# Four interleaved attention layers on one core: a new table of orders, engines and PSUM banks

## The chip, the cores and the metric

The kernel runs on one core of a Trainium2 chip. The core has five engines that run side by side, each through its own list of instructions in order: TensorE (PE in the profile; its weight loads are PEld), VectorE (DVE), ScalarE (ACT), GpSimd (POOL) and SyncE (SP, which here only issues DMAs). They wait for one another through semaphores. PE writes to PSUM, which has eight banks; DVE and ACT read PSUM and write SBUF; POOL works in SBUF alone. The metric is the device time of one execution in microseconds, as the median of several runs.

## What is computed

The input x has 2048 tokens of 512 features. Four residual layers follow one another, A, B, A, B, each on a layernorm of x. All have 32 heads of 16 features.

```python
def _A_ref(x, wqkv, wo):                      # linear attention
    q, k, v = ...                             # x @ wqkv, split into heads
    phi = lambda t: jnp.where(t > 0, t + 1, jnp.exp(t)) + 1e-6
    pq, pk = phi(q), phi(k)
    kv = jnp.einsum("bhsd,bhse->bhde", pk, v)
    z = jnp.einsum("bhsd->bhd", pk)
    num = jnp.einsum("bhqd,bhde->bhqe", pq, kv)
    den = jnp.einsum("bhqd,bhd->bhq", pq, z)[..., None] + 1e-6
    return (num / den) @ wo

def _B_ref(x, wqkv, wo):                      # sliding window, W = 256
    q, k, v = ...
    scores = jnp.einsum("bhqd,bhkd->bhqk", q, k) * (Dh ** -0.5)
    mask = (i - j >= 0) & (i - j < W)
    p = _softmax(jnp.where(mask, scores, -1e9))
    return jnp.einsum("bhqk,bhkd->bhqd", p, v) @ wo

x = A_x
x = x + _A_ref(_layernorm(x), A_wqkv, A_wo)
x = x + _B_ref(_layernorm(x), B_wqkv, B_wo)
x = x + _A_ref(_layernorm(x), A_wqkv, A_wo)
x = x + _B_ref(_layernorm(x), B_wqkv, B_wo)
```

## The kernel before

The tokens are cut into 16 tiles of 128. The residual stream stays in SBUF (`xres`) from the first load to the last store. `Plan.build` (L236) writes the whole program down as a graph of 2532 operations (`Graph.add`); an operation is one instruction, or a group of matmuls that goes by one name. Each names the engine or engines that may run it, what it reads and writes, and the PSUM tiles that it uses. A tile of PSUM is one bank.

The program has these parts, and work of one part is mixed with that of its neighbours:

- *First layer A, keys* (`layer_a_keys`): for each tile the layernorm (`norm`, L330 to L334: statistics on DVE, the inverse root in two POOL instructions, the scaling `xn` on DVE), a transposition, the key matmuls (`k`, L369) and phi: exponential on ACT (L392), two DVE instructions (L393, L394). Gram matrices of keys and inputs are summed over all 16 tiles (L444). Queries (`q`, L383) go through phi as well.
- *Barrier* (`barrier`): the sums over all tiles are complete (`kvm`, L486), the matrix M that joins them with the output weights is formed, and the denominators (`den`, L506; `rec`, L510; `recb`, L511; `spread`, L519; `pqd`, L526) are divided out.
- *First pass* (`middle(2)`): for each tile the output of layer A (`aout`, L369) is added to the residual (`res`, L537), normalised, transposed, and the layer-B queries, keys and values are made (`bq` and `bk`, L383; `bv`, L369; their copies `bqe`, L358, `bke`, L554 on ACT and L555 on DVE, `bve`, L358). Keys and values are laid out anew by two DMAs each (`kd`, L563; `vd`, L582). Then attention: scores of near blocks (`b_scores`, L599, 256 queries wide, two head groups at once), exponentials on ACT (`ex`, L609, 128 x 1024) and the diagonal mask on DVE (`mk`, L615); scores of the far edge (`b_far`, L632), exponentials (L641) and the edge mask (`mf`), either on POOL (L649) or on DVE (L650); values (`b_values`, L674), division (`rcp`, L685; `div`, L686), transposition of the output (`oT`), output matmul (`bout`) and residual. Keys and values (`a_k`, `a_v`, with the copy `ve`, L358) of the second layer A are made as its input appears.
- *Second barrier* and *second pass* (`middle(3)`): the same for layers three and four. Finished tiles leave by DMAs on POOL's queue (L783), the last by SP's.

The table's layernorm and output transposes are DMAs on SP's queue (L340) but for the first tiles of a part and the last one, which PE transposes through PSUM (L346) and ACT or DVE copies (`Te`, `oTe`, L353).

A score group uses four PSUM tiles at once, two for each of its two exponentials; an exponential reads two banks in one instruction.

What sets the order is a table. `place` (L88) decodes `TABLE` (L795): two bytes for each of the 2532 places give the operation that stands there in one global order, then one byte for each operation its engine, then one byte for each PSUM tile its bank. Each engine runs its operations in the global order; `synchronise` (L123) adds the semaphore waits that the dependencies need, among them that a tile that takes a bank comes after all uses of the tile that held it. So the table fixes every queue, SP's and POOL's too. The lines that pick an operation's place, engine and bank are these:

```python
order = [ops[raw[2 * k] + 256 * raw[2 * k + 1]] for k in range(n)]
o.eng = ("PE", "ACT", "DVE", "POOL", "SP")[raw[2 * n + o.i]]
x.banks = [raw[3 * n + k]]
```

Of the kernel before, what the change touches and what calls it, by code (L numbers as in the profile page):

```python
# [11 lines left out]
P = 128  # L12
D = 512
DH = 16
S = 2048
T = 16
# [196 lines left out]
class Plan:  # L213
# [372 lines left out]
    def b_scores(self, j, b, fs, key):  # L586

        K = self
# [4 lines left out]

        def put(e):
            m = None
            for i, f in enumerate(fs):
                for gq in range(4):
                    rows = slice(32 * gq, 32 * gq + 32)
                    m = e.matmul(K.ps(ps[gq])[:, ns * i:ns * i + ns], K.kB[rows, j % 4, 2 * f + b, :, :], K.XQ[rows, f, q:q + ns], start=True, stop=True, tile_position=(32 * gq, 0))  # L599
            return m  # L600
# [5 lines left out]
        for h in range(2):  # L606
            def ex(e, h=h):
                i = bass_view(K.PS[:, ps[2 * h].banks[0], :], [[512, 2], [ns, n], [1, ns]])
                return e.activation(out(2 * h, 2, ns), i, ACT.Exp, bias=0.0, scale=0.25)  # L609

            self.on("ACT", "ex", ex, key + 0.01 * h, act(2 * ns * n), wr=[("P", sl, f, b, h) for f in fs], rd=[("P", sl, f) for f in fs], ps=[ps[2 * h], ps[2 * h + 1]])
# [7 lines left out]
    def b_far(self, j, key):  # L619
# [3 lines left out]

        def put(e):
# [171 lines left out]
    r"c-rk(1Jq?nlFo<>WR`8)wr$(CZQHhO+qP|2wQYCpd+)ER>6z)7?d|Q|b9PU~|G&KV2EL5=B3_<%jfrF;8#GZ(6a&T@Hqi{3=q9BR6T`$bsZ44U",  # L796
    r"%cL=}O&pWf#5L)Rnmi_+NpJF+_@=$dVDg##CZkDUI+#JGqse3{nyIFk>0}C+X(qENXq-uCN}435kntv|8Emqc#wMKEX_}bCX1SSenwo4TndxkX",
    r"m>Fh;X=b{ZT_(IaZL*uLCWk3yikrgbuIXlSn&zgv*=_EbnI@6xVa}LbW|qlnhMJY;7gNr(Fsn>YGt8VdtIcq8-?TKn%tvO88DYws(xxPwGb7C?",
    r"6B&w_*=CO!ZO)rH=2w&4d~7b52d0l1W9FK@rnebuJ~1!NJ~PjJYSx;EX1-ZxN|<q`j7bXX%_FnGj5h{0n9s~YlMFVRYUXou(PW29X1^(GqQGU7",
    r"!W=N0%@vaz4w_OB6|S1crZhY;Dd3O+Xbgu<4TG@BJT*tmQIis)!58M4Nd>u0eRJJBHx*13^QCEJu9+9+D^tmof#_i2YZC)<Kuz<FA!uzFaza^n",  # L800
    r"$FwoIpd1J^fp1M)lN(ZlLLHL_(m*>?*QAB-jDrZKDWrqSCOyQ2dL|b1HMLD_=x5?Ud8lRjo48N`JWPa&kQWA+d=MWhK~Xc%#Do0M$Yg{JP#Gqe",
    r"MP{)n01Zq*SYir6LsJ+gnn`A<X$F&EnW+jbpbFH5de9MS!(_9?R5w#h9jI!ynodw3wwVUd5E{XD(;1GL=FkOpn3m8Ux<M;w3+<pQw1(rR4RnAT",
    r"=7i}1lVJ*UhovwTmcdDL2ByKg<}56SZE({}hf`(-yl1w<Ot@uMz${n^=U_Ihg73|0m;*bYC%kVKz#7;IYhfWAhudZm?1Emf8&1F;SPXOFB-}Cc",
    r"Afo9FKbXBRAI?J`*attFjnEG^!8-WBEP<cQX1D--;Ua{CQ*a4BH0vQ8{%peIWe5-b;R;m12rvK+!3H=C5g`I@fk$uzDq<vf0!Lv#RKf#r8XiML",
    r"{1C3fRyYVB!$)uzjzJ`>jFIskM8Rut1*771xDTH~G`xzR!&A5cpFkD73D@v5cnDST8C1htFbN;P3#g8h@eX_e@o@@1hZL9quVX5Vj_*JXjDZO;",
    r"B__d`*bozAGQ5F}a4O!0FJT}w#-un62f@4W6*R@^7z<}$226yhF*e@BjF=p6;d_t?;$SAs4DZ8COoLy;Ec^hnKwA6;vfyAyhjlP3WX1IO6V%0Q",
    r"P!qFZW^9J_uogDK7ML9uV{Kf5&G9yN!ljr4?_g)li7oMG$c0_-7s!pRups^lv#~YK!I$t9+u&UM7M`KOt{4vizlXbs_#ETnJ^T(VcEkHP4+(qV",
    r"4=^7KVO#8udGJRljP)@eR)Zqg0INe@EQ;;0J=TB)xB_cJ0w{((u{f^64p;ygYk}ZO?1%}W1S+n<)z}O3<610<z0qMQT!#;^5B9}Gum#uSVBCO-",
    r"VJmLKB(M=ZF2jeo376w$e1t<_JC??wPzIyfvKZYChY?T?ci=E60y{B=9fIX?DDJ|dFbs>qhZxh=wjbectYc%@;TYTQ!H+SH9f8GRFV?jq@mm~)",
    r"`*4AcYrn@55YH~O`|&%hXWzx-_9%XW@8Kdl8sEo$xY$0mi*Skk0Y}18`wrH(&ujxb3I<?*Y-q<|3LD>kfXi%3`y~#<WB4^bw}bFFCa_=O2|R#}",  # L810
    r"?5B7TM?+(~+<t?fVM2QdGuY4ZG5&}zY({$+U*Jjn2{YLz_ywl1@7SMlEWT?O;xCxij>98pZF74HGu!ca8gtn9Y&zS*PQcW5BA&sVHkD0p6WRA|",
    r"V%yT@vU%)T%wm(+y!ISswfSsEo6R<{*=;AA+cvfNE!k$av+ZixcC!Vn*e<raJ&$TH;IG)jUc`bnnSF_uu#LTpZLP6|th0S>Ve4%>8_t%r8*P6J",
    r"c9ZRA2U@i4ZFt+$4zerk0K3`tvV-k5o7DEUrR;V)#73~CZ6CYCma)6+P}{+lwY%*a`++TIciOeKyxn6f*dlhF9cGK#y>_J?ZY$bi_K+Q6E7?`{",
    r"h>d7V*wr?Y9cK^QG4Q1=ZpT7o`<2~lCqOFt+HSF_X*{&D<KURBY+KtX_JmDCRcusS)sD2s?T5CSU2m(~kL(6J+NP!Pc7jbuAKRlgJ)N@??I@dp",
    r"+EWM0NEhrR`-#m&pW2i5yxnIf+p%_vooe^nj`W%R$zHNw*aP;IJ!pTno#?dv#eQec*ex{8cBb#`S-X|G(69Eg%}rzMHu}NlAxn8F8%?)NUFk=g",
    r"ox0IWOLWoZpl__wb~4nR9POaYw3C25Wg(<p^tlx(Kw0UE{ni$ut2P|Xum$OwooS2Ebvw(3r=oPj&bBvg1e#-S*<w_IBGNY$i3(Fi>P^L|58bwv",
    r"s0`h)ed${&OC{(#ia{l*GL@t6X(;ue;gpZcQ&0MVO3{y$pLSCf8b&`+Y3fB)X(UynyS6%wrV(_{)}@~*CXJ$46q)YZ*ffB0QWSb%2hu}(l=e_m",
    r"8brq^4o#)wRF4MJ7@9_LDH_G2TvVSP+4wY_hENT9Y!gsTicSe>u5Cc`Y%MxK4XHmJr1`cEO{9L*hz`+Mnnb_Q6FZI?(+rwSP3RPjr@b_RPSX@h",
    r"MEmFrC8qs!j*?JQnn`Er0yU$gG>ekadAdcj3HT(<q1%Lfkrq*H61IGYu95Nyx<Sq9E;(*N*Xa^nrj~S*!gDKHOjjr(U!^6~nj&yyUP||98Aav$",
    r"w4Czs3W~xHXeGtwhm@Zq@pFp9tLRrMz%MB-&!yF5I62Luc$|WwaU1eHpHfnMK0<9N0WYMpe3;tNIZnur=mjkx=Ew97CE{?rhTf$ow3dk9qxX3o",  # L820
    r"CFc(~I<Kdc{60OS4RoGUa18!{I&n<?kUr$%9E(5V#9We}(#M>HOK@RM%}Kc+cjjbVgwyaf?!wo(D3{{${1I)W3j8q@<4shWEAnP4!-Y5%-{8tz",
    r"mM?H6uFB>3BH!dHe2IJWE$+kB_!GL#pHg4$&T08G>c>6#bNYnS@fXyCKjrjXoj>Cm+>0~taPG?e`Ewr0HTer3z#}*#*Wye(m<MtL&dguZARfx2",
    r"_$$i7mw5<(O<8#<U*Y9k!w%zRT${V`3a)9davdJcb$JXo<gr}KHsXa`pU3fH9?xI$B5ustxE^QcCY*ztGRQ`5#$WMf&dJSr32$PQuek-U<=p%Y",
    r"uj7`yh4b)w{+1_jUf#eHITugj?|3VJ&y#r@ujC*2N1no~cq(t_X}p75@oH|*cX&Fl;TilB-{pI}ldUwD`@D-E@NVA2E#x8Z<<|U&_i-DZ$1}MD",
    r"&*#UypWE^QCOOE5cow(g!#tax@DYB>3z+37pW<UYhv)KfKF!a#BR}U8e3D=A8GeV~<@fk!ZYFspkNm>L<X0{t;ib4lkfQRE3rPtv5>Z47O96=_",
    r"`6RNGl>DMnN(zdT($Z2|Nf~J^V`ZGglr~aUdP^T^E90e|#FF;XSC&W==^*{2qb!w9;w7r|mkBaJVoNs}D9fa~Oq9+tNG3@S2`7VPvUHK2GDPA?",
    r"Ihi6|rI!qqxDri<NqLzn!)1g_laW$EmP<t$CDCQNtdJ_QQpU(CsVp;OmduvXGE*wae5oo6WR9$sW3o{0$Xq!gG32f+lC5%F?#VpaCEMh_ES5bI",
    r"MYqcuiK@Hhft-?u5=}plM{-)CYZ)!8XC#K6lusq5K9&z9mX^~e@|k=t@g%m!m-3oecF0GvRuV`Yt)Tm4uT<1^@`db|N}5nM$a>i+N#uZ>m8bHt",
    r"B$8*6R1V5Uc`lb^lN^#{a#*fNa@i~|<Q+L8Tja7Fl`rL8`9$LCR}xRJ%KLIouE}|cuV2fLazPU4Mfq7OYf`-~-$*k3NfK&uttN@|S4pYW#b_1%",
    r"R=$(8@{7Ebbn?BtCpDz5{vhcEG?k{%dYVB}Yeu;tH>JL&QPEq1npjoSs@1AW>NK6QR@3mBUTdh=>RMAXXf~~-Q#FT9(~KHUhv;<8u8nl4HqlI)",  # L830
    r"Q-^70ZLGsJmqySmnny=yR*k45b(E%%+!{$!%4jX5sU)wC(d?31a!6!NBl)z57S`IDUz=)9X{H6Vffm(F(n1?*X2~T5^|mC@+|pdzX&oJ_?X`op",
    r")Z%(pi|IH$r&*+?bky-$N6za6tt%6?mSmMqI!SBG9__5zWUqG761q=kX-VC$v-NW=rC;bA?W(=Bw0^1eq>oP416p6Y=@dPvy>*@*(yz3YF3`E!",
    r"TEEuA`i*wiBicZ|)%n^++v+m?PSdy*+Cyh(PfhC<Y7_UpF4umV&Rx=`F1@>=i?qM?)n;z7Ue*k5l`heln$aEAmAYCpxutqco4XUbMq9XRdR$w&",
    r"liJGN(5pH?*Xlq$rPp<n4$>d=jBe4J`lGgXr*)lXcAIsu{-pPGz24Vt`m=7(3;IBR(T#dhAL*|O?ul+!bhq@eS|=`xd#Jb7xu?2S^SV2#?yiP&",
    r"`CNGSO!K=o?zu*AwcHD3m({(awOvG)&3&Za?a(?dyL(r6D!KQxo{Qvmsd4XXEca5|x;U<#`%ojh_Aa*T=c2gXn!`nP{asGi)zx*m+yEENb#u|(",
    r"#~Rmtpxxak8p9=WpK1q}$0czcT}+qTeWvkTCzse2a`D|jSJ)+R1zl2C#1(S|TtZjEC3g*_s7vM=NpaU$=C~$O&dqgArMz3~=DBsQf-C8Ix%sY?",
    r">+Ke}^{%vA==!)tu97R`Qn=1;v8&=zy0UJG>+7z#RIaj{<gU7ku8T|Urno`wnj7pUyQ*%RyY8yF?QV!0>Z-dNZil<+M!BA@hP&mQuj$4(?{B-Q",
    r"ZmGND!uio|m|Nz;`w?!MTj6@R<!+@L?l!qqu87~_#=4?@wTs|Kx`_U%tM7KYNPe^1=Zg7f?tmNTwz}tTyxZ?0`*&S&AI0x-@3{%CgrDekyOREW",
    r"SISR!huj`_*X?zOU1@*M9dv7419#sYai`n{_knBZHoDU;sz2%)xoG~3`_?sf(fu*^y*uvCxd-k$cf!5nzH}$uL-)d+bzi#~?!0^CX1cH3hi;aO",
    r";XiVZ-48CN|Hj4jv)#uomjBho^Do^e?nhU~$M-)u<J0+{T^#?Z`^9DO=s$DmeIgG&f&bi9^<TKeKB2$hF1n2ViA&;>`Ag3FYCeT8>#O^6KDJNp",  # L840
    r"lln})yszLh`-(oL@8c`^EWVcS>udW|KCAEN>-b!rd}W{8v#;x`_|#r}9^cHT@#?erw7!MU?(_QQzMik?bNHOTfv@3P`O7Z9Z|xWRmVSxP=iB)D",
    r"exPsb+xbDhp>OY(`oVsz@8BExj((hP?8p0|zKI{;hxh`1xG(4@_@=&)ALhIJiGGqF;n(>7zOY~GNBYTrlwaqk_)dPbpXxjNF@C+D=DYY6e!5@g",
    r"d-xfCrSIx{`gy*WU*%`|ZhpC+<#+hizPI1tcln)uqo3`!_)UJZ-|FZ1qkgyF=I8slet|#kxBFv$p+D*O_|yJ`Kjkm_Gk&kX<QMtN{;J>S&-(rT",
    r"n!oO^_yhi&zu|BC^ZtUr<?s62{+_?%ANc$Jp?~Bb`-A?8KjfeJr~a^i?vHr-JFx-5z}s5jrP>(4z!JKIso-~1_CJw7hVoA;`oFFLfY5DFFj!&m",
    r"FTiSG3CKTR(S)G{z29&W_$PX;q2E#9E5$##VMq~Jf@y?OLHx&i{JR*$zsLO}2=;#%0seCYi~n7OKf(k2`yBqc3ivNm@jHe536S66^LOS4{>y~?",
# [168 lines left out]
```

## Time and profile before

| | |
|---|---|
| median of three runs | 431.54 us (431.0 to 432.18) |
| span of the profiled execution | 428.2 us |
| mean granted TensorE clock in it | 0.986 |
| PE busy | 392.7 us (92%), 7471 matmuls recorded |
| DVE busy | 356.2 us (83%), 796 instructions |
| ACT busy | 347.4 us (81%), 433 |
| POOL busy | 128.6 us (30%), 223 |
| first near exponential of the first pass | starts at 69.04 us |
| first near exponential of the second pass | starts at 269.68 us |

The span runs from the first to the last instruction of the profiled execution; the runs' times also take in what lies around it. How busy each engine is over the span, in 40 equal slices, tenths of a slice, with the granted TensorE clock below:

```profile
PE   8899999999899999999999999999889979997775
...
DVE  6998899998998799887887789998798699875564
ACT  2423547999899999999998164999999999999992
POOL 4789322101240233130503303212144324332000
PEclk9999999999999999999999999999999999999968
```

ACT's row shows the parts of the program: it fills up when the first pass begins, about slice 7, falls off at slices 22 to 24, the second barrier, and is full again until the end. [...]

Waits are read from the list of who waited for whom; the longest on the engines that compute, apart from POOL's, are these (engine, line, what ended the wait: total us, times, longest):

```profile
ACT tE L392 <- PE ps L369: 20.6, 19, 2.2
DVE rc L685 <- PE ps L674: 15.0, 29, 1.5
PEld ps L599 <- ACT pb L609: 14.9, 31, 1.3
ACT tE L392 <- PE ps L383: 14.0, 10, 3.8
DVE pb L615 <- ACT pb L609: 11.6, 21, 2.1
```

### The profile page before, as it was taken

What the parts mean: (1) busy time and instruction counts of PE and PEld (TensorE: products, weight loads), DVE (VectorE), ACT (ScalarE), POOL (GpSimd) and SP (SyncE); (2) the same over time, 40 slices, a digit from 0 to 9 for tenths busy, and PEclk for the clock granted to TensorE, in tenths of its full rate; (3) what the DMA queues carried; (4) which work ended last, traced back from release to release, by engine and by line L of the source; (5) the groups of instructions that cost most, each with busy time, mean ns of one, the idle gap of its engine ahead of it and who ended that gap; (6) DMA issues with size and microseconds to landing.
All of it is one profiled execution on the core that took longest, in us unless ns stands there. A gap on an engine that the chain in (4) does not pass through costs nothing.

```text
span 428.2 us, 17035 instructions
## 1 busy us (share of the span) xinstructions
PE 392.7 (92%) x7471; PEld 257.9 (60%) x7548; DVE 356.2 (83%) x796; ACT 347.4 (81%) x433; POOL 128.6 (30%) x223
## 2 busy tenths in 40 slices
PE   8899999999899999999999999999889979997775
PEld 3445676766465566565565768585657746765544
DVE  6998899998998799887887789998798699875564
ACT  2423547999899999999998164999999999999992
POOL 4789322101240233130503303212144324332000
PEclk9999999999999999999999999999999999999968
DMA  7933016432153533453324000452434522553222
GB/s 248 269 74 87 2 42 160 117 90 70 39 111 64 103 103 77 91 112 55 95 47 65 19 2 26 114 120 63 113 62 106 116 77 77 116 133 102 64 52 51
DMA packets 66978, 37.81 MB, mean 88 GB/s; under 512 B 48248, under 2 KB 61816, under 8 KB 66904
## 3 DMA queue, kind: packets, MB, share of 16 engines
q1 hardware_dynamic: 66176, 34.75, 34.7%
q0 software_dynamic: 720, 1.97, 1.3%
q8 instruction: 59, 0.97, 1.0%
q14 instruction: 15, 0.12, 0.1%
q10 hardware_dynamic: 8, 0.00, 0.0%
HBM read 6.29 MB, written 2.10 MB: 20 GB/s over the span
## 4 chain that ended last, share of the span: by engine, by line
PE 42%; ACT 35%; DVE 16%; issue 4%; DMA 3%; POOL 1%; POOLq 0%; ACTq 0%
ACT pb L609 23%; PE ps L369 14%; PE ps L383 11%; PE ps L674 7%; ACT pb L641 6%; PE ps L599 4%; ACT vp L609 3%; DVE stats L330 2%; DVE XQ L526 2%; DVE vp L394 2%; ACT tE L392 1%; DVE tE L393 1%; DVE vp L334 1%; DMA xT<-xn 1%; DVE xres L537 1%
## 5 line engine op out<-in xcount | busy, mean ns | idle before, releaser
L609 ACT ACTIVATE pb<-ps 128x1024 bf16<-128x1024 f32 (+2 forms) x224 | 207.0, 1039 | 7.5 <-PE ps L599 6.1
L674 PEld LDWEIGHTS ps<-vB,pb 128*128 128x128 bf16 x2560 | 78.0, 96 | 13.0 <-DVE pb L615 2.8
L674 PE MATMUL ps<-vB,pb 128*128 128x34 bf16 x2560 | 83.6, 178 | 2.0 <-DVE pb L615 1.1
L392 ACT ACTIVATE tE<-ps 128x512 bf16<-128x512 f32 x64 | 38.8, 609 | 41.0 <-PE ps L369 20.6
L383 PE MATMUL ps<-xT,wBp 128*128 128x128 bf16 x1024 | 69.5, 219 | 2.1 <-DMA xT<-xn 0.8
L332 POOL TENSOR_SCALAR ve<-mv 128x1 f32<-128x1 f32 x64 | 16.6, 260 | 174.0 <-DVE mv L331 172.4
L383 PEld LDWEIGHTS ps<-xT,wBp 128*128 128x128 bf16 x1024 | 58.9, 98 | 14.8 <-issue 3.6
L615 DVE TENSOR_TENSOR pb<-pb,tri 128x512 bf16<-128x512 bf16 x112 | 48.0, 436 | 12.3 <-ACT pb L609 11.6
L599 PE MATMUL ps<-XQ,kB 32*128 32x256 bf16 (+2 forms) x1024 | 50.1, 270 | 6.9 <-ACT pb L609 3.4
L641 ACT ACTIVATE pb<-ps 128x1024 bf16<-128x1024 f32 x50 | 49.4, 1061 | 1.1 <-PE ps L632 1.0
L369 PE MATMUL ps<-wA,XQ 128*128 128x512 bf16 x177 | 46.3, 380 | 3.6 <-DVE vp L394 0.7
L537 DVE TENSOR_TENSOR xres<-ps,xres 128x512 bf16<-128x512 f32 x63 | 43.0, 685 | 7.3 <-PE ps L369 6.4
L649 POOL TENSOR_SCALAR_AFFINE_SELECT pb<-pb 128x1024 bf16<-128x1024 bf16 x30 | 35.3, 1175 | 38.5 <-ACT pb L641 37.3
L330 DVE BATCH_NORM_STATS2 stats<-xres 128x6 f32<-128x512 bf16 x64 | 43.1, 680 | 2.6 <-DMA xres<-in_A_x_dram 2.0
L333 POOL TENSOR_TENSOR rs<-ve,negh 128x1 f32<-128x1 f32 x64 | 37.5, 586 | 5.3
L383 PE MATMUL ps<-XQ,wA 128*128 128x128 bf16 x512 | 36.1, 219 | 0.4 <-DVE vp L394 0.2
L599 PEld LDWEIGHTS ps<-XQ,kB 32*128 32x128 bf16 x1024 | 15.5, 92 | 33.8 <-ACT pb L609 14.9
L369 PE MATMUL ps<-M,XQ 128*128 128x512 bf16 x115 | 31.7, 381 | 4.0 <-DVE XQ L526 1.6
L383 PEld LDWEIGHTS ps<-XQ,wA 128*128 128x128 bf16 x512 | 30.6, 98 | 7.7 <-DVE vp L394 1.2
L369 PE MATMUL ps<-wBo,oT 128*128 128x512 bf16 x104 | 30.1, 395 | 3.4 <-ACT pb L609 0.9
L369 PE MATMUL ps<-wBv,xT 128*128 128x512 bf16 x106 | 30.7, 381 | 2.7 <-issue 0.8
L369 PEld LDWEIGHTS ps<-wA,XQ 128*128 128x128 bf16 x192 | 16.1, 98 | 21.5 <-ACT XQ L353 1.7
(109 smaller groups left out, 541.2 us busy)
## 6 DMA issues: line engine op xcount, KB each, us to landing
vB<-vS SPq DMA_DIRECT2D x64, 136.0 KB, 2.5
kB<-vp SPq DMA_DIRECT2D x64, 128.0 KB, 2.2
out_dram<-xres POOLq DMA_DIRECT2D x15, 128.0 KB, 2.3
wA<-in_A_wqkv_dram SPq DMA_DIRECT2D x3, 512.0 KB, 5.9
xres<-in_A_x_dram SPq DMA_DIRECT2D x2, 512.0 KB, 4.9
pb<-in_B_wqkv_dram SPq DMA_DIRECT2D x1, 1024.0 KB, 9.0
xres<-in_A_x_dram SPq DMA_DIRECT2D x3, 256.0 KB, 4.9
wAo<-in_A_wo_dram SPq DMA_DIRECT2D x1, 512.0 KB, 7.4
```

The lines of the kernel that those rows point to most:

```text
L330: self.on("DVE", "stats", lambda e: e.bn_stats(K.stats[:, t, :], K.xres[:, t, :]), key, dve(512), rd=[("xres", t)], wr=[("stats", t)])
L333: self.pow = self.on("POOL", "pow", lambda e: e.tensor_tensor(K.rs[:, t, :], K.ve[:, t, :], K.negh[:], ALU.pow), key + 0.03, (640, 690), r ...
L369: m = e.matmul(K.ps(ps), lhs(c), rhs(c), start=c == 0, stop=c == 3)
L383: m = e.matmul(K.ps(ps)[:, f * P:(f + 1) * P], w(c, f), xT(c), start=c == 0, stop=c == 3)
L392: self.on("ACT", "E", lambda e: e.activation(K.tE[:, s, :], K.ps(ps), ACT.Exp, bias=0.0), key, act(512), wr=[("tE", s)], ps=[ps])
L537: self.on("DVE", "res", lambda e: e.tensor_tensor(K.xres[:, t, :], K.ps(po), K.xres[:, t, :], ALU.add), key, dve(512), rd=[("xres", t)], w ...
L599: m = e.matmul(K.ps(ps[gq])[:, ns * i:ns * i + ns], K.kB[rows, j % 4, 2 * f + b, :, :], K.XQ[rows, f, q:q + ns], start=True, stop=True, ti ...
L609: return e.activation(out(2 * h, 2, ns), i, ACT.Exp, bias=0.0, scale=0.25)
L615: return e.tensor_tensor(x, x, K.tri[:, 0, :].unsqueeze(1).unsqueeze(1).to_broadcast([P, 4, n, 64]), ALU.mult)
L641: return e.activation(far(h), i, ACT.Exp, bias=0.0, scale=0.25)
L649: return e.affine_select(out=x, in_=x, compare_op=ALU.is_ge, fill=0.0, base=-2, pattern=[[0, 16], [-2, 64]], channel_multiplier=1)
L674: m = e.matmul(K.ps(ps)[:, 34 * u:34 * u + 34], K.P((b // 2) % rp)[:, gq, f, o:o + P], K.vB[:, (b // 2) % 4, b % 2, r, :], start=i == 0, s ...
```

## The change

The whole `TABLE` is replaced by another one of the same form: another global order, other engines for 41 operations that may run on more than one, and other PSUM banks. The graph of operations, their instructions and their dependencies through data stay. Engines change so: the far-edge mask from DVE to POOL 15 times and from POOL to DVE 10 times; the copies `Te` (3), `bqe` (2), `Me`, `bve` and `oTe` (1 each) from DVE to ACT; `ve` (3), `bke` (2), `ge` and `recb` (1 each) from ACT to DVE. After it ACT has 433 operations of the graph for 432, DVE 789 for 795, POOL 224 for 219; PE and SP keep theirs.

Besides, the exponentials of `b_scores` and `b_far` no longer assume that their two banks lie side by side: a small function `pair` takes the distance from the table, and the far exponential's output is written with one dimension more.

```diff
@@ b_scores
+        pair = lambda two, free: bass_view(K.PS[:, two[0].banks[0], :], [[512 * (two[1].banks[0] - two[0].banks[0]), 2]] + free)
...
             def ex(e, h=h):
-                i = bass_view(K.PS[:, ps[2 * h].banks[0], :], [[512, 2], [ns, n], [1, ns]])
+                i = pair(ps[2 * h:2 * h + 2], [[ns, n], [1, ns]])
                 return e.activation(out(2 * h, 2, ns), i, ACT.Exp, bias=0.0, scale=0.25)
@@ b_far
+        pair = lambda two, free: bass_view(K.PS[:, two[0].banks[0], :], [[512 * (two[1].banks[0] - two[0].banks[0]), 2]] + free)
...
-        far = lambda h: bass_view(K.P(sl)[:, 2 * h, 0, 256:320], [[704, 8], [384, 2], [1, 64]])
+        far = lambda h: bass_view(K.P(sl)[:, 2 * h, 0, 256:320], [[2816, 2], [704, 4], [384, 2], [1, 64]])
         for h in range(2):
             def ex(e, h=h):
-                i = bass_view(K.PS[:, ps[2 * h].banks[0], :], [[128, 8], [64, 2], [1, 64]])
+                i = pair(ps[2 * h:2 * h + 2], [[128, 4], [64, 2], [1, 64]])
                 return e.activation(far(h), i, ACT.Exp, bias=0.0, scale=0.25)
@@ module
 TABLE = (
-    r"c-rk(1Jq?nlFo<>WR`8)wr$(CZQHhO+qP|2wQYCpd+)ER>6z)7?d|Q|b9PU~|G&KV2EL5=B3_<%jfrF;8#GZ(6a&T@Hqi{3=q9BR6T`$bsZ44U",
...
+    r"c-qxi1Gp_ol8%Us$jE%QZQHhO+qP}nwr$(C{o1y>-_|*|dv|B2r*~$yzuDb7=T>D!2L3-HGEdb7hy?~>Lo^_W4rw7B!~ldi5EtS>0Z0!SAR`FGhXjxiG",
...
```

In the old order SP issues the input and weight loads as x0, x1, key weights (A), x2-3, x4-5, query weights (A), x6-7, x8-11, x12-15, value weights (A), output weights (A), layer B's query and key weights, then the first transposes; in the new one as x0, x2-3, x1, key weights, x4-5, x6-7, query weights, x8-11, the first transpose, x12-15, layer B's query and key weights, value weights, then further transposes, with the output weights of A among them.

## The prediction

> **What bounds the kernel now.** I read the page's totals first, then busy time by stretch, then the chain that ended last, then single lines. I cut the span where ACT's work changes: to the first exponential of the first attention pass (69 us), its last (235), the first of the second pass (269.5), its last (419.3).
>
> ```profile
> 69.00:235.00 166.00, 156.10 (x3159) 101.12 (x3191) 145.12 (x332) 157.79 (x190) 41.46 (x68) 1.00 0.38 84
> 235.00:269.50 34.50, 33.34 (x566) 25.61 (x569) 29.27 (x67) 15.06 (x27) 8.13 (x15) 1.00 0.09 25
> 269.50:419.30 149.80, 134.83 (x3052) 91.60 (x3072) 117.15 (x255) 145.78 (x168) 40.29 (x57) 0.97 0.39 93
> ```
>
> Columns: stretch, length, then busy us (instructions) of PE, PE's weight loads, DVE, ACT, POOL, then clock, DMA share, GB/s. ACT is busy 95% of the first attention pass and 97% of the second, and idles over half of the boundary between them, where PE is 97% busy. ACT sets the passes, PE and DVE the rest. The chain agrees, except that PE takes over in the second half of the first pass:
>
> ```profile
> PE 42%; ACT 35%; DVE 16%; issue 4%; DMA 3%; POOL 1%; POOLq 0%; ACTq 0%
> ```
>
> The main ACT work and the price of an exponential:
>
> ```profile
> L609 ACT ACTIVATE pb<-ps 128x1024 bf16<-128x1024 f32 (+2 forms) x224 | 207.0, 1039 | 7.5 <-PE ps L599 6.1
> ...
> L599 PEld LDWEIGHTS ps<-XQ,kB 32*128 32x128 bf16 x1024 | 15.5, 92 | 33.8 <-ACT pb L609 14.9
> ```
>
> Exponentials of 1024 columns take 1.06 us each but start 0.90 us apart when back to back (the chain of waits has "126.17 7.34 ACT pb L609 x8", 0.92 each); a break costs the idle time and some 0.16 us of lost overlap. Score matmuls in turn wait 14.9 us for ACT to free PSUM banks: the loop score, exponential, free bank, score is tight on both sides.
>
> **The change part by part.** Both tables were read out beside each other (two bytes an operation for the order, one for its engine, one a tile for its bank). All 2532 operations stay. Of 858 PE groups 435 keep their predecessor on the engine, of 795 on DVE 197, of 432 on ACT 131, of 219 on POOL 81, of 228 on SP 31; 816 of 997 bank numbers change. 41 operations change engine. The sum goes by what this moves into or out of the bounding stretches.
>
> *The access patterns.* In both tables every pair of score banks is adjacent (all 156 groups), so the new stride equals the old 512, and the far output [2816 x 2][704 x 4] is the same walk as [704 x 8]. Cost nil; nothing need hide it. If the extra dimension cost 10 ns in each of 312 exponentials, they being the bound, it would be 3 us.
>
> *ACT's work inside the passes.* Prices are start-to-start times of back-to-back rows: about 0.49 us for a phi exponential, 0.61 for L554's key copy, 0.48 for L358's plain copies, 0.54 for the V copies, 0.20 for L511. First pass: one phi exponential fewer (-0.49), one key copy fewer (-0.61), three layer-A value copies fewer (-1.43), two query copies (+0.96) and one V copy (+0.54) more: -1.0 us. Second pass: one key copy (-0.61) and L511 (-0.20) fewer: -0.8. The boundary gets +1.7 us of ACT work, hidden by PE (ACT is busy 15 of 34.5 us there); uncovered it would cost 1.7. **Term -1.8.**
>
> *Score groups with little cover.* For each group I counted the ACT work ordered between the exponential that frees its last bank and the one that reads it. With a whole exponential or more between, the trace shows 0.03 us of idle a group in the first pass; with half, 0.17; with none, 0.55 (second pass 0.02, 0.09, 0.40). Counts, first pass: none 4 to 6, half 20 to 10, whole 47 to 52: +1.10 - 1.69 + 0.13 = -0.46. Second pass: none 3 to 2, half 6 to 7, whole 66 to 69: -0.40 + 0.09 + 0.05 = -0.26. Eight breaks fewer at 0.16 each: -1.28. **Term -2.0**; bounds 0 (what is no longer ACT's wait becomes PE's) and -4.
>
> *DVE, and masks to POOL.* L650 masks on DVE (0.60 us start to start) become L649 on POOL 15 times and the reverse 10 times, net five, so DVE sheds 3.0 us in all, 2.9 of it in the first pass after the other swaps. DVE holds 16% of the chain: 2.9 x 0.16 = -0.5. Against it stands what POOL's mask does to DVE:
>
> ```profile
> L649 POOL TENSOR_SCALAR_AFFINE_SELECT pb<-pb x30: 1136/1147/1659, 98.7 to 381.9; 128x1024 bf16<-128x1024 bf16 x30
> ...
> L334 DVE TENSOR_SCALAR xn<-xres,mv,rs x48: 320/405/1239, 58.0 to 369.5; 128x512 bf16<-128x512 bf16 x48
> ...
> L615 DVE TENSOR_TENSOR pb<-pb,tri x112: 359/416/1376, 73.2 to 415.2; 128x512 bf16<-128x512 bf16 x112
> ```
>
> Durations are minimum, median and maximum in ns. The 1239 ns L334 and the 1376 ns L615 began beside a POOL mask: three L334 then took 1.2 us for 0.40, some L615 0.8 to 1.4 for 0.42, two L393 0.6 and 0.8 for 0.28. All such stretching, twelve cases in the timeline, sums to 6.9 us over 35 POOL masks, 0.20 each. At that rate five more masks cost 1.0 us of DVE. Laying each mask at its place in the orders, DVE operations of these kinds that begin beside one go from 19 to 45; at 6.9 / 12 = 0.57 us for each of 26 more that is 15 us of DVE. On the path at DVE's 16%: +0.2 to +2.4; uncovered at most +15. Placement in an order is rough, so I take +0.7. **Term, both: +0.2.** The Trainium skill ("SBUF — State Buffer", Who interferes with whom) says that one of them that takes the shared port pair holds it for its whole instruction and the other fully blocks, for a DVE operation with two SBUF inputs or in a two-port mode; "Perfetto Trace Analysis", Optimizing Scalar/DVE Operations, warns that offloading between the two might not help. Taken literally, moving a 0.60 us mask onto a 1.15 us one that can block DVE is a loss, and this term would be near its upper end; the trace, where most POOL masks stretch nothing, makes it small.
>
> *Transposes with less cover.* SP's transposes (L340) land at best 2.4 us after their input is ready, in the middle 3.0, in a quarter of cases over 4.0:
>
> ```profile
> L340 SPq DMA_TRANSPOSE xT<-xn x28: 1189/1256/2755, 60.1 to 379.0; - x28
> ...
> DMA to landing us min/median/max: 2.4/2.6/5.1
> ```
>
> I counted the work of the busiest engine ordered between the release of a layernorm transpose (its input and everything that SP queues ahead) and the first matmul that reads it. Before, the shortest is 3.3 us and five are under 4.0. After, four are under 3.0 (2.4, 2.4, 2.6, 2.8) and eleven under 4.0. Against a 3.0 landing the shortfall is 0.6 + 0.6 + 0.4 + 0.2 = 1.8; against 4.0 it is 8.9 where it was 2.0, 6.9 more. Three of the four lie where PE holds the chain, but the matmuls have some slack behind other work as well; I take half, **+0.9**; bounds 0 and +6.9. Queued behind a late one on PE are the next token tile's matmuls, and behind them ACT. The attention outputs' transposes get longer cover (under 4.0: 3 to none), which offsets some.
>
> *The head.* PE work ordered before the first scores goes from 54.4 to 54.0 us and DVE's from 54.0 to 53.7, so -0.3. But on SP the key weights now come behind another 256 KB of input, about 1 us at the 270 GB/s of the first 20 us, and the loads of tiles 12 to 15, of layer B's weights and of layer A's value weights stand behind the first transpose. The other input loads run ahead of it and DVE begins on them; bounds -0.3 to +1.5, **term +0.2**. In the tail PE's last 26 groups are the same but for one score group; nil.
>
> **Sum:** -1.8 - 2.0 + 0.2 + 0.9 + 0.2 = -2.5. The profiled span is 428.2 us; the runs have 431.0 to 432.2, so 3.3 lie around it at the median and are unchanged. 428.2 - 2.5 + 3.3 = **429.0 us**.
>
> **Rivals.** *Larger gain.* The passes lose 316 us of stretch less 293.5 us of ACT work at back-to-back prices (151.4 and 142.1), 22 us. The bank numbers now rotate over all eight (66% of score tiles lay in the first four, now 54%), so waits could shrink also where I count equal cover. If four tenths of the 22 went: -9, 422.5 us. For it: cover rises in the first pass. Against: in the second it doesn't. *No change:* in the second half of the first pass the chain is PE's, and PE's work there is 141.2 us in both; ACT's relief goes nowhere, -0.8 in the second pass is left, transposes give it back: 431.5. *Slower: transposes late on SP.* Short cover at 33, 129, 156, 162, 171, 227 and 240 us stalls PE's queue with DVE's xn (L334) stretched by POOL masks just before. At the 4.0 us landing, +6.9 instead of +0.9, with DVE at -0.5 + 2.4 and the score term at nil: -1.8 + 1.9 + 6.9 + 0.2 = +7.2, so 438.7; it decides against the change, other terms as forecast, once late transposes cost over 3.4 us. For it: before, no transpose had such short cover, and all PE waits on them sum to about 2 us. Against: in the passes PE has 10 to 15 us of slack behind ACT.
>
> **How the numbers follow.** Forecast 0.42, larger gain 0.17, no change 0.11, slower 0.30. A measurement can tell 0.3%, about 1.3 us, from none. Nearly all of the forecast case lies beyond that: faster 0.58, same 0.12, slower 0.30. The forecast's own range is 425 to 430; the range to reach eight in ten goes from 420.5 to 436.
>
> **What would show it.** Right: ACT idle before L609 under 6 us; ACT busy 1 to 2 us less in the passes; PE's idle before L383 and L369 for a transpose at 3 us or less. Wrong: more than 5 us of such waits; L334's mean well over its 446 ns with L649 beside it; the first exponential later than 70 us; or a chain in which ACT's share rises though its work fell.

## The result, and the profile after

| | before | after |
|---|---|---|
| median of four runs | 431.86 us (431.0 to 433.36) | 443.52 us (442.75 to 447.94) |
| ratio, 95% interval | | 1.029 (1.0234 to 1.0345) |
| span of the profiled execution | 428.2 us | 439.9 us |
| mean granted TensorE clock | 0.986 | 0.984 |

The new table is 2.9% slower. The forecast was 429.0 us with a range to 436; the time lies outside it, beyond the rival that had the transposes late (438.7). Medians here and below are of all runs; two of the kernels with loads moved had one run each in a slower state of the chip, which their ratios leave out.

Inserted lines move the numbers: the near exponential L609 is now L611, its scores L599 L601, the diagonal mask L615 L617, the far exponential L641 L645, POOL's mask L649 L653, the values L674 L678, the division L685 and L686 L689 and L690. First the busy time by stretch of the kernel after, cut at its own first and last near exponentials (columns as in the prediction):

```profile
0.00:70.39 70.39, 63.22 (x632) 37.16 (x633) 59.80 (x136) 27.81 (x49) 36.44 (x80) 1.00 0.49 123
70.39:241.21 170.82, 161.70 (x3222) 102.91 (x3221) 146.95 (x324) 156.95 (x187) 51.22 (x76) 0.99 0.36 82
241.21:276.46 35.25, 33.79 (x548) 25.04 (x544) 30.67 (x64) 17.33 (x32) 7.80 (x15) 1.00 0.08 24
276.46:430.70 154.24, 138.52 (x3068) 91.24 (x3068) 120.85 (x258) 145.71 (x166) 39.90 (x56) 0.98 0.41 91
```

Against the stretches before, the head is 1.4 us longer, the first pass 4.8, the boundary 0.8, the second pass 4.4. ACT's work in the passes fell by 0.9 us and its idle time rose: 170.8 - 157.0 = 13.9 us in the first pass (8.2 before), 154.2 - 145.7 = 8.5 in the second (4.0). DVE works 3.7 us longer in the second pass (120.85 for 117.15), in three instructions more. The chain that ended last, by engine:

```profile
PE 45%; DVE 23%; ACT 13%; DMA 9%; POOL 5%; issue 5%; SPq 0%; POOLq 0%; DVEq 0%
```

ACT held 35% of it; now 13%. DVE went from 16 to 23, DMAs from 3 to 9, POOL from 1 to 5. The exponentials still do the most work, but they are fed late. Their group, and that of the far mask on POOL (busy time, mean ns, then idle time before and what ended most of it):

```profile
L611 ACT ACTIVATE pb<-ps 128x1024 bf16<-128x1024 f32 (+2 forms) x224 | 208.3, 1023 | 15.9 <-PE ps L601 14.5
...
L653 POOL TENSOR_SCALAR_AFFINE_SELECT pb<-pb 128x1024 bf16<-128x1024 bf16 x37 | 44.7, 1209 | 30.0 <-ACT pb L645 28.3
```

ACT waits 15.9 us before L611 where it waited 7.5. In the list of waits PE's weight loads wait less for ACT's banks (12.9 us for 14.9): the loop between scores and exponentials is a little less tight from that side. The waits of interest in the kernel after (`XQ` holds the transposed inputs of layer A, `xT` those of layer B, `oT` the transposed attention outputs), and the row of the page for PE's matmuls on `XQ`:

```profile
ACT pb L611 <- PE ps L601: 14.5, 25, 1.6
PEld ps L601 <- ACT pb L611: 12.9, 23, 1.6
...
PE ps L383 <- DMA xT<-xn: 2.9, 5, 0.9
...
PE ps L369 <- DMA oT<-o: 1.6, 2, 1.3
...
L369 PE MATMUL ps<-wA,XQ 128*128 128x512 bf16 x192 | 48.5, 380 | 5.1 <-DMA XQ<-vp 2.7
```

PE's matmuls now wait 2.7 + 2.9 + 1.6 = 7.2 us for transposes (7.5 with the smaller entries), where it was 1.4; PE's weight loads wait for the same landings. Layer B's transposes land no later than before:

```profile
L340 SPq DMA_TRANSPOSE xT<-xn x28: 1190/1270/2517, 60.5 to 395.6; - x28
...
DMA to landing us min/median/max: 2.4/2.5/4.6
```

Their worst case went from 5.1 us to 4.6, so what is short for them is the cover. The attention outputs' transposes have the median that they had too (2.5 us for 2.6), but the longest takes 5.5 us for 4.1. The other view that moved is that of single DVE lines (minimum, median, maximum in ns):

```profile
L334 DVE TENSOR_SCALAR xn<-xres,mv,rs x48: 321/403/1328, 58.3 to 390.0; 128x512 bf16<-128x512 bf16 x48
...
L393 DVE TENSOR_SCALAR tE<-tE x64: 229/282/1976, 9.6 to 319.1; 128x512 bf16<-128x512 bf16 x64
...
L617 DVE TENSOR_TENSOR pb<-pb,tri x112: 360/415/1390, 74.9 to 427.0; 128x512 bf16<-128x512 bf16 x112
```

Medians are as before, maxima are not rare any more: 22 DVE instructions beside one of the 40 POOL masks are stretched, that is, they take longer than the median of their kind, by 15.4 us in all (11 of L617, 5 of L334, 4 of L393, 2 masks on DVE). Before it was 12 instructions and 6.9 us beside 35 masks. Two places of the timeline of the kernel after (start, length, engine, line, and in brackets the idle time before it with what ended it):

```profile
310.98 1.98 DVE L393 TENSOR_SCALAR tE<-tE 128x512 bf16<-128x512 bf16 x1 [0.45 <-ACT tE L392]
312.99 0.69 DVE L394 SCALAR_TENSOR_TENSOR XQ<-ps,tE 128x512 bf16<-128x512 f32 x1
313.59 0.25 DVE L689 RECIPROCAL rc<-ps 128x16 f32<-128x16 f32 x1
313.88 0.42 DVE L690 TENSOR_TENSOR o<-ps,rc 128x256 bf16<-128x256 f32 x1
...
311.63 2.38 POOL L653 TENSOR_SCALAR_AFFINE_SELECT pb<-pb 128x1024 bf16<-128x1024 bf16 x2
...
314.36 0.40 PE L601 MATMUL ps<-XQ,kB 32*128 32x256 bf16 x8 [1.58 <-DVE o L690]
...
314.81 1.94 ACT L611 ACTIVATE vp<-ps 128x1024 bf16<-128x1024 f32 x2 [1.49 <-PE ps L601]
...
383.04 1.72 DVE L617 TENSOR_TENSOR pb<-pb,tri 128x512 bf16<-128x512 bf16 x2
...
383.35 2.42 POOL L653 TENSOR_SCALAR_AFFINE_SELECT pb<-pb 128x1024 bf16<-128x1024 bf16 x2
```

The first place is the loss in small: L393 takes 1.98 us for its 0.28, so phi, reciprocal and division behind it on DVE are 1.7 us late; PE, whose next scores wait for that division, stands still for 1.58; ACT, which waits for those scores, for 1.49. (L393 begins ahead of the recorded start of the mask, beside a POOL store's issue; spans on POOL are rough.) At 383 us two diagonal masks take 1.72 us for 0.83, the second lying wholly beside POOL's mask.

### The profile page after: what moved, and what is told of

It is laid out like the page before. It is cut to its first block, busy times and chain, and to the rows that moved or that the text cites. A ratio compares the mean times of both kernels' runs of the same rounds, so it can differ in the third digit from the quotient of the medians.

```text
span 439.9 us, 17188 instructions
## 1 busy us (share of the span) xinstructions
PE 401.9 (91%) x7548; PEld 259.5 (59%) x7548; DVE 362.1 (82%) x790; ACT 348.7 (79%) x434; POOL 135.9 (31%) x228
## 4 chain that ended last, share of the span: by engine, by line
PE 45%; DVE 23%; ACT 13%; DMA 9%; POOL 5%; issue 5%; SPq 0%; POOLq 0%; DVEq 0%
PE ps L369 16%; PE ps L383 11%; PE ps L678 9%; ACT pb L611 7%; PE ps L601 5%; DVE stats L330 3%; DVE xres L537 3%; ACT vp L611 3%; DMA xT<-xn 2%; DVE pb L617 2%; DMA oT<-o 2%; DVE xn L334 2%; ACT pb L645 2%; DVE tE L393 2%; DVE XQ L526 2%
## 5 line engine op out<-in xcount | busy, mean ns | idle before, releaser
L611 ACT ACTIVATE pb<-ps 128x1024 bf16<-128x1024 f32 (+2 forms) x224 | 208.3, 1023 | 15.9 <-PE ps L601 14.5
L678 PEld LDWEIGHTS ps<-vB,pb 128*128 128x128 bf16 x2560 | 78.0, 96 | 16.6 <-issue 6.2
L678 PE MATMUL ps<-vB,pb 128*128 128x34 bf16 x2560 | 83.0, 178 | 5.2 <-DVE mv L331 1.6
L332 POOL TENSOR_SCALAR ve<-mv 128x1 f32<-128x1 f32 x64 | 15.7, 245 | 203.7 <-DVE mv L331 202.9
L392 ACT ACTIVATE tE<-ps 128x512 bf16<-128x512 f32 x64 | 37.9, 606 | 32.3 <-PE ps L369 16.5
L601 PE MATMUL ps<-XQ,kB 32*128 32x256 bf16 (+2 forms) x1024 | 50.4, 272 | 9.4 <-ACT pb L611 2.6
L617 DVE TENSOR_TENSOR pb<-pb,tri 128x512 bf16<-128x512 bf16 x112 | 51.9, 468 | 3.2 <-ACT pb L611 2.8
L653 POOL TENSOR_SCALAR_AFFINE_SELECT pb<-pb 128x1024 bf16<-128x1024 bf16 x37 | 44.7, 1209 | 30.0 <-ACT pb L645 28.3
L369 PE MATMUL ps<-wA,XQ 128*128 128x512 bf16 x192 | 48.5, 380 | 5.1 <-DMA XQ<-vp 2.7
L645 ACT ACTIVATE pb<-ps 128x1024 bf16<-128x1024 f32 x50 | 49.4, 1054 | 1.9 <-PE ps L636 1.8
L333 POOL TENSOR_TENSOR rs<-ve,negh 128x1 f32<-128x1 f32 x64 | 38.3, 598 | 5.3
L601 PEld LDWEIGHTS ps<-XQ,kB 32*128 32x128 bf16 x1024 | 15.7, 93 | 36.8 <-ACT pb L611 12.9
L369 PE MATMUL ps<-wBo,oT 128*128 128x512 bf16 x124 | 34.5, 388 | 2.7 <-DMA oT<-o 1.6
L369 PE MATMUL ps<-wBv,xT 128*128 128x512 bf16 x128 | 35.1, 381 | 0.9 <-ACT vp L611 0.5
L369 PE MATMUL ps<-M,XQ 128*128 128x512 bf16 x128 | 33.2, 381 | 1.7 <-DVE XQ L526 0.8
L383 PE MATMUL ps<-XQ,wA 128*128 128x128 bf16 x512 | 34.6, 219 | 0.1
```

The costliest lines, as they stand in the source:

```text
L333: self.pow = self.on("POOL", "pow", lambda e: e.tensor_tensor(K.rs[:, t, :], K.ve[:, t, :], K.negh[:], ALU.pow), key + 0.03, (640, 690), r ...
L369: m = e.matmul(K.ps(ps), lhs(c), rhs(c), start=c == 0, stop=c == 3)
L383: m = e.matmul(K.ps(ps)[:, f * P:(f + 1) * P], w(c, f), xT(c), start=c == 0, stop=c == 3)
L392: self.on("ACT", "E", lambda e: e.activation(K.tE[:, s, :], K.ps(ps), ACT.Exp, bias=0.0), key, act(512), wr=[("tE", s)], ps=[ps])
L617: return e.tensor_tensor(x, x, K.tri[:, 0, :].unsqueeze(1).unsqueeze(1).to_broadcast([P, 4, n, 64]), ALU.mult)
L645: return e.activation(far(h), i, ACT.Exp, bias=0.0, scale=0.25)
```

## The experiments

Ratios are against the kernel before, run beside each on the same chip; its medians there were 431.2 to 432.2 us.

**The access patterns alone.** The new code of `b_scores` and `b_far` over the old table.

> The new access patterns with the old table. If the patterns cost nothing (all score banks stay adjacent, so the addresses are the same), 431.5 us within 0.3%. If the fourth dimension of the far output costs ACT 10 ns or more an exponential, 432.5 to 435.

431.36 us, ratio 0.9991 (0.9959 to 1.0023). They cost nothing, so all of the loss is the table's.

**Waits for transposes taken out, in both kernels.** Matmuls whose input a DMA on SP's queue transposes read part of a weight instead, so they compute from other data; the transposes are still issued. Such a matmul waits no longer for its tile's load and layernorm either, so the edit prices everything that reaches PE through a transpose, and not the DMA alone. For keys it reads so, and in the same way for the other users:

```diff
 def a_k
+        q = ("XQ", t) in K.viaq
-        xT = lambda c: K.XQ[:, c, t * P:(t + 1) * P]
-        ps = self.tok("k", t, xT, lambda c: K.wA[:, c, 512:1024], [("XQ", t), ("wAk",)], key)
+        xT = lambda c: K.wA[:, c, 512:640] if q else K.XQ[:, c, t * P:(t + 1) * P]
+        ps = self.tok("k", t, xT, lambda c: K.wA[:, c, 512:1024], ([] if q else [("XQ", t)]) + [("wAk",)], key)
```

> The old table, but every matmul that would read a tile transposed by a DMA reads a part of a loaded weight instead, so the layers' keys, queries, values and outputs come from other data; the transposes are still issued. It prices PE's waits for transposes in the old order. PE's waits for them sum to 1.8 us in the profile: 429.5 to 431.5.

> The same edit with the new table (matmuls read a part of a loaded weight where they would read a tile transposed by a DMA). Theory T: PE's 8.6 us of waits for transposes go, and with them most of the 11.7 us of loss: 433 to 437, within 4 us of the same edit on the old table. Theory P: DVE is stretched as before, 440 to 443. If a third cause leads (less cover between exponentials and scores on PE's queue: ACT idle before L609 7.5 us before, 15.9 after), 439 or more with ACT's idle time before the exponentials still above 12 us.

Before: 430.16 us, 0.9959 (0.9929 to 0.9988). After: 437.16, 1.0109 (1.0052 to 1.0166). The waits are worth 6.4 us in the new order and about 1.3 in the old. The difference, 5.1 us, is under half of the loss, so the transposes are one cause and not the only one.

**POOL's masks taken off the port, in both kernels.** "The port" is the shared pair of ports that the prediction speaks of. Each mask on POOL becomes two one-column instructions of the kind and length of L333 (0.6 us each), so that part of the mask is left out. POOL's queue, its waits and its busy time stay; the wide reads and writes of SBUF go.

```diff
 def b_far, mk
-                    return e.affine_select(out=x, in_=x, compare_op=ALU.is_ge, fill=0.0, base=-2, ...)
+                    e.tensor_tensor(y(0), K.rs[:, 0, :], K.negh[:], ALU.pow)
+                    return e.tensor_tensor(y(1), K.rs[:, 0, :], K.negh[:], ALU.pow)
```

> The old table, with each far-edge mask on POOL replaced by two instructions of the kind of L333 (one column each, 0.59 us, as long together as the mask), so that part of the mask is left out; DVE instructions beside L333 ran at their usual times in the profile of before. It prices the stretching of DVE in the old order: 6.9 us of stretching go, of which DVE's share is small: 428 to 431.5.

> The same edit with the new table (each POOL mask replaced by two one-column instructions of the same time, so part of the mask is left out). Theory P: 15.4 us of DVE stretching go, and 4 us or more of time, 439 or less. Theory Q (score groups and copies wait because the new banks are freed by DVE, whatever its speed): 441 to 443.5.

Before: 431.11 us, 0.9984 (0.9958 to 1.001). After: 436.06, 1.0095 (1.0063 to 1.0128): 7.5 us less than the change itself. Single lines, groups and chain of this edit over the new table:

```profile
L617 DVE TENSOR_TENSOR pb<-pb,tri x112: 360/415/456, 77.8 to 423.1; 128x512 bf16<-128x512 bf16 x112
```

```profile
PE 44%; ACT 20%; DVE 16%; DMA 9%; issue 5%; POOL 4%; SPq 1%; POOLq 0%; DVEq 0%
...
L611 ACT ACTIVATE pb<-ps 128x1024 bf16<-128x1024 f32 (+2 forms) x224 | 207.8, 1027 | 8.2 <-PE ps L601 6.9
```

The longest L617 is now 456 ns where it was 1390, ACT's idle time before its exponentials falls from 15.9 to 8.2 us, and DVE's share of the chain is back at the 16% of the kernel before. The L393 that took 1.98 us at 311 takes 0.32 here. DMAs keep their 9%.

**Both edits at once, in both kernels.** They leave only what the orders, banks and copies do by themselves.

> Old table, both edits (matmuls read a part of a weight for a transposed tile; POOL masks replaced by two one-column instructions). The level against which the new table with both edits is read: 427 to 430.5.

> New table, both edits: no matmul waits for a DMA transpose (they read a part of a weight) and no POOL mask beside DVE (two one-column instructions in its place). The no-wait edit alone gave 437.2. If transposes and stretching are the whole loss, 429 to 432, within 2 us of the same edits on the old table. If Q has a share of its own, 434 to 437.

Before 429.46 us, 0.9945 (0.9918 to 0.9971); after 429.28, 0.9944 (0.9922 to 0.9965). The four medians of each order side by side:

| us | as it is | no transpose waits | masks off the port | both |
|---|---|---|---|---|
| old table | 431.5 | 430.16 | 431.11 | 429.46 |
| new table | 443.52 | 437.16 | 436.06 | 429.28 |

With both edits the tables are equal, and the effects add up: 6.4 + 7.5 = 13.9 of 14.2 us. The four runs of the new table as it is lie between 442.75 and 447.94 us, and the interval of its ratio is some 2.4 us wide to each side, so a figure that is a difference from 443.52 is good to 2 or 3 us; that the two kernels with both edits agree rests on 10 and 7 runs and is good to about 1 us. The passes of the two, in busy time by stretch, the new table first:

```profile
68.81:233.35 164.54, 154.87 (x3188) 102.05 (x3221) 140.19 (x324) 156.32 (x187) 49.80 (x98) 1.00 0.40 85
...
268.60:417.17 148.57, 135.08 (x3043) 91.59 (x3068) 114.05 (x258) 144.63 (x166) 39.45 (x74) 0.97 0.39 94
```

```profile
68.85:233.64 164.79, 155.58 (x3158) 100.85 (x3190) 142.57 (x332) 157.26 (x189) 39.96 (x84) 1.00 0.40 85
...
268.48:418.02 149.54, 135.87 (x3041) 92.13 (x3068) 113.61 (x255) 145.31 (x168) 39.21 (x76) 0.94 0.38 93
```

The passes of the new table are 0.25 and 0.97 us shorter (the second at a granted clock of 0.97 for 0.94), and the theory falls that the new rotation of banks costs time by itself, unless a gain of the same size hides it. With both edits ACT holds 40% of the chain under the new table and 38% under the old.

**The masks' engines put back.** The new order and banks, with the 25 far masks on their old engines, as it is and with POOL's masks off the port.

> The new table, but the 25 far-edge masks that changed engine go back to their old one (35 on POOL, 21 on DVE, as before). Theory P (POOL's masks stretch DVE: 6.9 us in the profile of before, 15.4 in that of after): stretching falls to some 7 to 9 us and the time by 4 to 8 us, to 436 to 440. Theory T (transposes land too late for PE; PE's waits on DMAs 1.8 us before, some 12 after): little changes, 442 to 444.

> The new table with the 25 masks on their old engines, which gave 450.5, and with POOL's masks replaced by two one-column instructions of the same time (part of the mask is left out). If the 450.5 came from stretching, as with the new engines (7.5 us), 441 to 443. If the masks' places in POOL's and DVE's queues cost it (PE waited 4.4 us for POOL masks in the second pass), 445 or more.

450.48 us, 1.0396 (1.0324 to 1.0468), and 443.84, 1.0283 (1.0221 to 1.0346). A miss: fewer masks on POOL were to help, and cost 7 us more. Stretching did fall, to 18 instructions and 10.4 us, and taking it out still brings 450.5 - 443.8 = 6.7 us, on intervals of some 3 us to each side. Off the port this kernel is 7.8 us slower than the new table with its own engines (436.06). That is laid here to the masks' places in the queues, of which the waits show a part: in the second pass PE's value matmuls wait 4.0 us in one piece for a mask on POOL, in the first 1.6 us for one on DVE. How many masks POOL has doesn't tell their price.

**The new engines in the old order.** All changed engines over the old order and banks, as it is and off the port; and the copies' engines alone, without the masks'. The two tables differ in 40 engines, of 25 masks and 15 copies, and the list under "The change" adds up to the same; 41 and 16 are miscounts.

> The old order and banks with the 41 new engine choices. My prediction had them at -1.8 us from ACT and +0.2 from DVE and POOL: 429.5 to 431. If engine choices only fit their own order, 433 to 440, with more stretching of DVE than the 6.9 us of before.

> The old order with all 41 new engines, and POOL's masks replaced by two one-column instructions of the same time (part of the mask is left out). With POOL's masks it had 436.4 and 12.6 us of stretching. If stretching is what cost, 429.5 to 432; if the copies or the masks' places in the queues, 434 or more.

> The old order and banks with the new engines of the 16 copies alone (masks as before). It tries my term of -1.8 us for ACT: 429 to 430.5 if moving copies off ACT in the passes pays; 431 to 432.5 if ACT's relief goes nowhere; 434 or more if it was these copies, and not the masks, that cost the old order with all 41 new engines its 4.9 us.

436.39 us, 1.0118 (1.0067 to 1.0168); 433.29, 1.0029 (1.0012 to 1.0045); the copies alone 434.19, 1.0068 (1.0044 to 1.0091). In the old order the new mask engines raise the stretching from 6.9 to 12.6 us, and taking it out gives 3.1. The copies, costed at a gain, cost 2.7 us. Group row and wait of the kernel with the copies alone:

```profile
L609 ACT ACTIVATE pb<-ps 128x1024 bf16<-128x1024 f32 (+2 forms) x224 | 207.4, 1041 | 10.9 <-PE ps L599 9.6
```

```profile
PEld ps L599 <- ACT pb L609: 16.3, 34, 1.3
```

ACT's near exponentials wait 10.9 us (7.5 before) and PE waits 1.4 us longer for ACT's banks: my reading, which no run takes apart, is that a copy that leaves ACT in one place makes DVE late there, and one that comes makes ACT late elsewhere.

**The loads in the head.** Five kernels ask why transposes are late there. The first takes out the transposes' waits for the first layer's keys and queries alone.

> The new table, with matmuls reading a part of a weight for a DMA-transposed tile in the first layer's keys and queries alone (so those come from other data). Everywhere it brought 443.5 to 437.2. In the profile of after 2.8 us of PE's 8.6 us of waits for transposes are in the head: if waits cost what they last, 440 to 441.5; if the head's cost has been made up by the end, 443; if it is nearly all of the effect, 437 to 438.5.

438.65 us, 1.0156 (1.0126 to 1.0186): 4.9 of the 6.4 us. All the other transposes are worth the 1.5 us from here to 437.16. The two profiled executions show less of it: the first exponential ends 2.5 us earlier, the first pass is 2.4 us shorter and the second 2.5 longer, which leaves 2.4 us of span (437.5 for 439.9). The profiled execution of the kernel after has the shortest span of its four runs (439.9 to 446.1), so where the other 2 us or so lie isn't seen. The chain of waits in order of time, in the kernel after, shows where the head stands still:

```profile
15.81 6.95 DMA XQ<-vp
22.80 1.47 PE ps L369 x6
```

Then the loads themselves. `x12-15`, layer A's value and output weights and layer B's query and key weights are moved ahead of SP's first transpose, as in the old order; the second kernel besides moves the layernorms and transposes of eleven tiles forward, until each has 4.4 us of work as cover.

> The new table with four loads (input tiles 12 to 15, value and output weights of A, query and key weights of B) moved ahead of the first transpose on SP's queue, as in the old table. In the profile of after the second transpose is issued at 15.7 us and lands at 22.6, behind the last of these loads, and PE waits 2.8 us for it. If those loads hold it up: that wait falls under 1 us, the first exponential ends near 70 us for 71 to 74, and the time falls by 1.5 to 3 us, to 440.5 to 442. If not, 443.5.

> The same, and in the new table the layernorm and the transpose of eleven more tiles whose cover was under 4.4 us stand earlier in the order (statistics to transpose, 4 places at a time, until 4.4 us of work lie between scaling and first matmul). Theory T, as the 2 by 2 of the edits has it (6.8 us for transposes): PE's waits for transposes fall from some 7 us to under 3, and the time to 437 to 440. If only the latency itself and not the order matters, 441 or more.

446.49 us, 1.0369 (1.0292 to 1.0446), and 459.59, 1.0629 (1.0557 to 1.0701): both misses. With the loads first the chain has one wait in place of the other:

```profile
12.73 9.62 DMA XQ<-vp
22.49 3.57 PE ps L369 x8
```

The first three transposes, issued at 12.7, 17.4 and 19.5 us, land at 22.4, 22.8 and 23.3, the last load at 21.9, and the first near exponential starts at 76.4 us for 70.4. More cover lowered the waits of PE's matmuls for the layernorms' transposes from 5.9 to 3.2 us, but those for the attention outputs' rose from 1.6 to 3.8, and the first pass, between the ends of its first and last near exponential, takes 179.5 us for 169.9 in the kernel after. DVE's share of the chain rose from 23 to 29%; that the layernorms now stand on DVE ahead of work that others wait for is the likely cause, and isn't shown apart.

The last two move loads the other way, behind the first four transposes: layer B's weights and layer A's value weights in the new table, and with layer A's output weights in the old.

> The new table with two loads on SP's queue (layer B's query and key weights, 1 MB, and A's value weights, 512 KB) moved behind the first four transposes. In the profile of after the transpose issued at 15.7 us lands at 22.6, 6.9 us later, where 2.5 are usual, among these loads' packets. If the loads' traffic holds the head's transposes up, it lands within 5 us, PE waits under 1 us for it, and some of the 4.9 us that the head's waits cost comes back: 439.5 to 442. If the wait is the order's own, 443.5.

> The old table with the same two loads and A's output weights moved behind the first four transposes, which land 3.5 to 4.5 us after their issue there. PE waits 0.6 us for them, so at most that is to be had if nothing else moves up: 430.5 to 431.5; a gain over 0.3% only if DVE and PE behind them use the earlier landing.

446.6 us, 1.0331 (1.029 to 1.0372), and 439.89, 1.0179 (1.0138 to 1.0219): misses too. In the new table the transpose that waited before is issued at 17.7 now and lands at 20.8; those issued at 27.0 and 28.3 land at 33.9 and 34.4, just after the last load at 33.4. But there the chain does not pass through them. It passes through POOL, which re-arranges layer B's weights (`wBp`, L316) and has the roots of two layernorms queued behind:

```profile
25.85 6.21 DMA pb<-in_B_wqkv_dram
...
32.20 0.76 POOL wBp L316
...
33.70 0.58 POOL rs L333
...
34.31 0.41 DVE vp L334
```

POOL waits 5.6 us for that load, and DVE 5.0 us for roots, 4.8 of it in one piece; so this kernel's loss isn't the transposes' alone. In the old table it is a transpose that stands in the chain; SP's issues and the chain:

```profile
25.06 0.58 SPq L259 DMA_DIRECT2D pb<-in_B_wqkv_dram  x1
25.69 0.50 SPq L259 DMA_DIRECT2D wA<-in_A_wqkv_dram  x1
26.23 0.51 SPq L259 DMA_DIRECT2D wAo<-in_A_wo_dram  x1
26.78 6.90 SPq L340 DMA_TRANSPOSE XQ<-vp  x4
```

```profile
26.78 7.48 DMA XQ<-vp
34.40 1.87 PE ps L369 x4
```

Three loads issued in 1.7 us, the transpose behind them lands 7.5 us after its issue, and PE's matmuls, which waited 0.5 us for `XQ` transposes in the head of the kernel before, wait 6.7, of which 6.4 in one piece. The first near exponential starts 8.1 us later (77.15 for 69.04), and the kernel is 8 us slower. A transpose issued under large loads is late, whichever of them it is; moving these loads changed which, and in the new table it also held up POOL.

No kernel that does the whole computation was faster than the one before.

## Why the prediction was wrong

By the table of both edits the 12.0 us between 431.5 and 443.5 are about 5.1 for what reaches PE through the transposes (the difference of their worth in the two orders: 6.4 - 1.3; 6.8 - 1.6 with the masks off the port), 7.1 for POOL's masks on DVE (7.5 - 0.4; 7.9 - 0.7 without transpose waits), and -0.2 for all the rest, the first two good to 2 or 3 us. Point by point:

- *The access patterns* at nil: right.
- *DVE, and masks to POOL*, +0.2, measured about +7.1: the largest error. The count pointed the right way (19 to 45 instructions begun beside a mask; "uncovered at most +15"; measured 8.5 us more of stretching, 6.9 to 15.4). What failed is the step "DVE holds 16% of the chain": a delay was multiplied by DVE's share of the old chain. A us of stretching removed is worth 7.5 / 15.4 = 0.5 us in the new order and 0.4 / 6.9 = 0.06 in the old, where it isn't clear of nothing (ratio 0.9984, 0.9958 to 1.001). The other two prices, 3.1 / 12.6 = 0.25 with new engines in the old order and 6.7 / 10.4 = 0.64 with old masks in the new, are too rough to be told from 0.5. So the price differs by order, and no share of the old chain could give it. What sets it is shown at one place, 311 us: what DVE has queued behind the stretched instruction, and who waits for that; for the rest it is argued. The Trainium skill's rule ("SBUF — State Buffer", Who interferes with whom) is that who takes the shared port pair first holds it for the whole instruction and the other fully blocks. The 0.4 us instructions that take 1.3 us beside a 1.15 us mask agree with it. The one-column instructions don't show such a hold: they read SBUF too and last 0.6 us, and of the 19 diagonal masks that began beside one in the new order none took over 456 ns. The rule's reading in the prediction, a term near its upper end, pointed the right way; that most masks stretch nothing in the old trace spoke of the old order only.
- *Transposes with less cover*, +0.9, and *the head*, +0.2: measured about +5.1, by the medians most of it in the head. The mechanism was named, the place was not: short cover was forecast at 33, 129 and more places up to 240 us, while the longest wait ends at 23 us. What failed is the head's step. It costed the loads by their place in SP's queue and their bytes ("about 1 us", bounds -0.3 to +1.5) and let the transposes among them land like any other; the two issued while the loads were under way landed 6.95 and 5.65 us after their issue, the first of them half a us after the last load (22.76 and 22.27 us). In the passes layer B's landings were no longer than before, and of the 6.4 us some 1.5 are left for them, as near to the 0.9 as can be told.
- *ACT's work inside the passes*, -1.8, and *score groups with little cover*, -2.0: with all else that isn't the other two costs, measured -0.2 together. That they brought something which another cost took back is not excluded. ACT's busy time did fall by 0.9 of the 1.8 us, but a copy moved is also work for the other engine, and in the old order the same copies cost 2.7. Cover counted in ACT's work shows no gain in ACT's waits either: its idle time before near exponentials, of both kinds of output tile, is 11.2 us in the new order without both costs and 9.8 in the old.
- *What would show it wrong* did: over 5 us of transpose waits, the first exponential after 70 us. But "a chain in which ACT's share rises" came out the other way, 35% to 13%: ACT lost the bound to what feeds it.
- *The sum*: ACT and the cover were 3.6 us too hopeful, DVE 6.9 short, transposes and head 4.0 short; together the 14.5 us between 429.0 and 443.5. The slower rival had the right two mechanisms, but DVE at its 16% again, so its 438.7 is 4.8 us short. That its 6.9 us for transposes came near the 5.1 is luck: they were late landings all over the passes, and the long wait was in the head.

## What to carry to other kernels

A share of the chain is no price for a delay: look at what is queued behind the delayed instruction on its engine, and who waits for that, since in the new order each us of it cost about half a us, and in the old next to nothing. Count as cover of a DMA only what is left after the transfers that are in flight when it is issued. Don't price an order and its engine choices apart: the new order lost 7 us more with the old masks' engines, and the new engines cost the old order 4.9.

## What the runs showed of the hardware

- The first DMA transpose issued behind the weight loads (0.5 to 1 MB each) on SP's queue, while these were under way, landed 0.5 us after the last of them in each of five orders: 6.95 us after its issue in the kernel after, 9.6, 6.9 and 7.5 with the loads moved, and 4.4 in the kernel before, where an undisturbed one takes 2.4 to 2.5.
- POOL's one-column instructions, placed where the 1024-column masks were and of the same total length, stretch none of the diagonal masks (maximum 456 ns in a kernel with 40 such pairs, where 19 masks began beside one); the wide mask stretches a DVE instruction to as much as 1.4 us for 0.4. POOL's memsets do it too: with the masks off the port the only long ones left behind the head, two L334 of 1.12 and 1.23 us and one L393 of 1.12, run beside 1 us memsets of 128 x 1024 and 128 x 1152.
- The costs of late transposes and of stretched DVE instructions are additive in one order as far as the runs can tell (6.4 + 7.5 for 14.2 us, each good to 2 or 3), and small in another with the same work (1.3 and 0.4 us).
